# Attention's triangles masked by TensorE in PSUM instead of by GpSimd behind the exponential

## The chip, the core and the metric

One core of a Trainium2 chip runs the kernel. The metric is device time in microseconds for one execution; before the change the median of three runs is 384.74 us (384.6 to 386.14).

## What is computed

The reference is a transformer block with two parts, both on one sequence of 2048 tokens of width 512. Only the attention part matters for this change:

```python
def _A_ref(x, wqkv, wo):
    H = 32; Dh = 16; W = 256
    q, k, v = ...                                  # x @ wqkv, 32 heads of 16
    scores = jnp.einsum('bhqd,bhkd->bhqk', q, k) * Dh ** (-0.5)
    idx = jnp.arange(S)
    mask = (idx[:, None] - idx[None, :] >= 0) & (idx[:, None] - idx[None, :] < W)
    scores = jnp.where(mask[None, None], scores, -1000000000.0)
    p = _softmax(scores, axis=-1)
    o = jnp.einsum('bhqk,bhkd->bhqd', p, v)
    return o.reshape(B, S, D) @ wo                 # heads side by side

h = _layernorm(x) * (1 + ca) + sa
x = x + ga * _A_ref(h, A_wqkv, A_wo)
h = _layernorm(x) * (1 + cb) + sb
x = x + gb * _B_ref(h, B_w1, B_b1, B_w2, B_b2)     # layernorm, matmul over tokens, gelu, matmul
```

Each query sees itself and the 255 keys before it. In blocks of 128 tokens, a block of keys is seen by three blocks of queries: its own (the lower triangle), the next one (all of it) and the one after that (the opposite triangle).

## The kernel before

The kernel runs in three stages. Up to 48 us it normalizes and transposes the tokens, makes V for all heads and Q and K for the first 8 of 32 heads. From 48 to about 246 us runs attention, in an order written out by hand (`tc.manual_schedule()`), and between its steps the Q and K projections of the other 24 heads. The rest adds the residual and runs the second part, where a scheduler sets the order.

Attention is cut into 96 units: 8 sets of 4 heads (hs), 4 groups of 512 queries (tg), 3 kinds (ui). A unit has up to three pieces of keys by queries, in UNITS: (key block, first query block behind it, number of query blocks, place in the tile). Together they fill 512 columns for each head, and 128 for kind 0 of the first group (tg 0). The scores of a unit's four heads are made in two halves, a = 0 and 1, each in a tile `pss` of two PSUM banks, one bank to a head; there are three such tiles. K of a head stands in 32 rows of KeT or KoT, so a score matmul uses 32 rows of the array, and the two heads of a half use different rows.

The exponential (`emit_exp`, ScalarE, L320) reads one `pss` of 128x1024 and writes half of `et`. GpSimd then zeroes the triangles in `et` (`emit_mask`, L335): two selects a unit, one for each of the two triangles, and one alone for kind 0 of the first group (no block behind the diagonal there); MASKED names the blocks. The values (`emit_av`, L352) come one unit later: four heads side by side, 32 columns of the array each, 512 columns of `et` for each head, into the tile `psb`. After kind 2 VectorE transposes `psb` (L362), divides by the sums and merges the heads.

The loop over units u puts on TensorE: scores of unit u + 1, half 0; where `fill` has one, half of a projection (two matmuls of 128x512 into another `psb`, L387); scores of u + 1, half 1; values of u - 1. A half of scores waits for the exponential that frees its `pss`. `fill` has 48 parts for the first 69 steps; after every second one VectorE copies the projection out (L393 for Q; L395 and twice L397 for K). There are two `psb` buffers for values and projections.

Of the kernel before, what the change touches and what calls it, by code (L numbers as in the profile page):

```python
# [10 lines left out]
ALU = mybir.AluOpType  # L11

P = 128
# [10 lines left out]
SCORE_SCALE = DH ** -0.5  # L24
GELU_C0 = 0.044715
GELU_C1 = 1.5957691216057308


@with_exitstack
def kernel(  # L30
# [14 lines left out]
    nc = tc.nc  # L45
# [17 lines left out]
    identity = const.tile([P, P], DT.bfloat16, name="identity")  # L63
# [8 lines left out]
        out=mask_even[:], in_=ident_v[:, :, 0, :], axis=mybir.AxisListType.XY, op=ALU.add,  # L72
# [3 lines left out]
        out=mask_odd[:], in_=ident_v[:, :, 1, :], axis=mybir.AxisListType.XY, op=ALU.add,  # L76
# [11 lines left out]
    with tc.tile_pool(name="modps", bufs=2, space=bass.MemoryType.PSUM) as modps:  # L88
# [31 lines left out]
        for v in range(2):  # L120
            for oc in range(ND):
                col = v * ND + oc
                for k in range(ND):
                    nc.tensor.matmul(
                        ps_fm[:, col : col + 1],
                        lhsT=wmod[:, k, v * D + oc * P : v * D + (oc + 1) * P],
                        rhs=sT[:, k : k + 1],
                        start=(k == 0), stop=(k == ND - 1),
# [113 lines left out]
    for v, dst, add1 in ((2, bc_ga, False), (4, bc_cb1, True), (3, bc_sb, False), (5, bc_gb, False)):  # L242
        ps_b = ps_big.tile([P, D], DT.float32, name="psb")
        for k in range(ND):
            nc.tensor.matmul(
                ps_b[:], lhsT=sT_rep[:, k, :], rhs=wmod[:, k, v * D : (v + 1) * D],
                start=(k == 0), stop=(k == ND - 1),
# [14 lines left out]

    MASKED = ((1, 4, 0), (1, 3, 1), (0, 3, 1))

    maskLD = const.tile([P, 4, P], DT.bfloat16, name="maskLD")
    nc.vector.memset(maskLD[:], 1.0)
    nc.gpsimd.affine_select(
        out=maskLD[:, 0:2, :], in_=maskLD[:, 0:2, :], pattern=[[0, 2], [-1, P]],
        compare_op=ALU.is_ge, fill=0.0, base=-1, channel_multiplier=1,
    )  # L270
    nc.gpsimd.affine_select(
        out=maskLD[:, 2:4, :], in_=maskLD[:, 2:4, :], pattern=[[0, 2], [1, P]],
        compare_op=ALU.is_ge, fill=0.0, base=0, channel_multiplier=-1,
    )

    wod = const.tile([P, ND, D], DT.bfloat16, name="wod")
# [1 line left out]
    for g in range(ND):  # L278
        dma.dma_start(out=wod[:, g, :], in_=wo_v[:, g, :])
    nc.vector.tensor_tensor(  # L280
        out=wod[:], in0=wod[:], in1=bc_ga[:].unsqueeze(1).to_broadcast([P, ND, D]),
# [3 lines left out]
    with tc.tile_pool(name="epool", bufs=4) as epool, tc.tile_pool(  # L285
# [4 lines left out]
        units = [(hs, tg, ui) for hs in range(8) for tg in range(NT // 4) for ui in range(3)]  # L290
        merge_tiles = [None] * 4
        state = {}

        def pieces(tg, ui):
            return [(4 * tg + kb, r0, nr, blk) for kb, r0, nr, blk in UNITS[ui] if 4 * tg + kb >= 0]

        def emit_scores(u, a):
            hs, tg, ui = units[u]
            g8, par = hs // 2, hs % 2
            Ksel = KeT[g8] if par == 0 else KoT[g8]  # L300
            pss = ps_s.tile([P, 2, 4 * P], DT.float32, name="pss")
            for kb, r0, nr, blk in pieces(tg, ui):
                for jj in range(2):
                    j = 2 * a + jj
                    rows = slice(32 * j, 32 * j + 32)
                    nc.tensor.matmul(  # L306
                        pss[:, jj, blk * P : (blk + nr) * P],
                        lhsT=Ksel[rows, kb * P : (kb + 1) * P],
                        rhs=QT[g8][rows, (kb + r0) * P : (kb + r0 + nr) * P],
                        start=True, stop=True, tile_position=(32 * j, 0),  # L310
                    )
            state[u, a] = pss

        def emit_exp(u, a):
# [6 lines left out]
                out=et[:, 2 * a : 2 * a + 2, b0 * P :], in_=state.pop((u, a))[:, :, b0 * P :],  # L321
                func=ACT.Exp, scale=SCORE_SCALE,
            )

        def emit_mask(u):
            hs, tg, ui = units[u]
            et = state[u, "e"]
            lo, hi, m0 = MASKED[ui]
            if tg == 0 and ui == 0:
                lo, m0 = 3, 2  # L330
            for b0, b1, diag in ((lo, lo + 2 - m0, False), (max(lo, lo + 2 - m0), hi, True)):
                if b0 >= b1:
                    continue
                nb, s = b1 - b0, 1 if diag else -1
                nc.gpsimd.affine_select(  # L335
                    out=et[:, :, b0 * P : b1 * P], in_=et[:, :, b0 * P : b1 * P],
                    pattern=[[0, 4], [0, nb], [s, P]], compare_op=ALU.is_ge, fill=0.0,
                    base=0 if diag else -1, channel_multiplier=-s,
                )

        def emit_av(u):
            hs, tg, ui = units[u]
# [60 lines left out]
        fill = [part for g8 in range(1, ND) for tg in range(NT // 4) for part in proj_parts(g8, tg)]  # L403
# [4 lines left out]
        for u in range(len(units)):  # L408
            emit_exp(u, 0)
            if u + 1 < len(units):  # L410
                emit_scores(u + 1, 0)
            evac = None

            if fill and (n_fill - len(fill)) * (3 * 24 - 3) <= u * n_fill:
                mms, evac = fill.pop(0)
                mms()
            emit_exp(u, 1)
            if u + 1 < len(units):
                emit_scores(u + 1, 1)
            if u > 0:  # L420
                emit_av(u - 1)
            if evac is not None:
                evac()
            emit_mask(u)
        emit_av(len(units) - 1)
        assert not fill

# [45 lines left out]
    with tc.tile_pool(name="xp2", bufs=3) as xp2:  # L473
        B1_LAG = 2
        for tb in range(NT):
# [3 lines left out]
            for g in range(ND):  # L479
                nc.tensor.matmul(  # L480
                    pa[:], lhsT=OTd[g][:, tb * P : (tb + 1) * P], rhs=wod[:, g, :],
                    start=(g == 0), stop=False,
# [13 lines left out]
                out=nb2[:], in0=mv[:, 0:1], scalar=-1.0, in1=rstd[:], op0=ALU.mult, op1=ALU.mult,  # L496
# [3 lines left out]
                out=xn2[:], in_=x2[tb][:], func=ACT.Identity, bias=nb2[:], scale=rstd[:],  # L500
# [14 lines left out]
                out=nb3[:], in0=mv3[:, 0:1], scalar=-1.0, in1=rstd3[:],  # L515
# [3 lines left out]
                out=hb[tb][:], in_=h2[:], func=ACT.Identity, bias=nb3[:], scale=rstd3[:],  # L519
# [14 lines left out]
    with tc.tile_pool(name="gtmp", bufs=2) as gtmp:  # L534
# [7 lines left out]
        for fg in fgroups[2:]:  # L542
            nfc = len(fg)
            pu = ps_u.tile([P, 2, D], DT.float32, name="pu")
            for sc in range(NT):
# [3 lines left out]
                for i, fc in enumerate(fg):  # L549
                    nc.tensor.matmul(  # L550
                        pu[:, i, :], lhsT=w1r[:, sc, fc * P : (fc + 1) * P], rhs=hb[sc][:],
                        start=(sc == 0), stop=(sc == NT - 1),
# [61 lines left out]
```

## Time and profile before

| | |
|---|---|
| median of three runs | 384.74 us |
| profiled execution, its own time | 385.87 us |
| its span, first to last instruction | 383.9 us |
| attention with projections | 48.4 to 197.2 us |
| attention without projections | 197.2 to 245.5 us |
| TensorE busy over the span | 337.2 us |
| ScalarE busy over the span | 256.5 us |
| GpSimd busy over the span | 156.2 us |

The span is the time from the first to the last instruction; the profiled execution's own time is 2.0 us longer. PE is TensorE's matmuls, PEld its weight loads, ACT ScalarE, DVE VectorE, POOL GpSimd. A matmul's duration in the rows holds its drain, which runs beside the next matmul; the pace of TensorE is therefore read from the starts of successive groups, not from durations. The granted clock is a share of 2.4 GHz; its two levels here are 1.00 (2.4 GHz) and 0.50 (1.2 GHz).

### The profile page before, as it was taken

How to read it: one execution, taken by the hardware profiler on the slowest of the kernel's cores; microseconds unless marked ns; L12 is line 12 of the kernel's file. 1: busy time of each engine (PE TensorE's matmuls, PEld its weight loads, DVE VectorE, ACT ScalarE, POOL GpSimd, SP SyncE). 2: the span in 40 equal slices, each digit the busy share in tenths (PEclk: the TensorE clock that was granted, in tenths of full speed). 3: DMA queues.
4: the chain of work that ended last, by engine and by line, in shares of the span. 5: the costliest groups of instructions: out<-in, count | busy, mean ns of one | idle time of the engine just before them, and what ended most of it. 6: DMA issues, size and time to landing. Idle time of an engine off the chain costs nothing.

```text
span 383.9 us, 6976 instructions
## 1 busy us (share of the span) xinstructions
PE 337.2 (88%) x2753; PEld 131.7 (34%) x2753; DVE 208.4 (54%) x508; ACT 256.5 (67%) x350; POOL 156.2 (41%) x208
## 2 busy tenths in 40 slices
PE   0798979999999789899998989889984999899992
PEld 0544432323333222232333334233431444344441
DVE  6695635656443443535463134399983985442144
ACT  3478389799797877787999999889974653200000
POOL 9000068687776665665877878600000000000000
PEclk9999985555555555555555555699998899999997
DMA  7980000000000000000000000069302960000111
GB/s 226 364 178 1 2 0 2 3 2 0 2 2 2 1 3 2 0 2 3 0 2 2 2 3 2 0 224 406 138 0 94 402 272 2 0 31 26 56 55 55
DMA packets 17160, 24.57 MB, mean 64 GB/s; under 512 B 5096, under 2 KB 12776, under 8 KB 17128
## 3 DMA queue, kind: packets, MB, share of 16 engines
q1 hardware_dynamic: 17128, 24.13, 18.1%
q8 instruction: 21, 0.34, 0.4%
q14 instruction: 11, 0.09, 0.1%
HBM read 22.03 MB, written 2.10 MB: 63 GB/s over the span
## 4 chain that ended last, share of the span: by engine, by line
PE 56%; DVE 19%; ACT 10%; issue 3%; POOL 2%; DVEq 0%; POOLq 0%; ACTq 0%
PE pss L306 13%; PE py L570 13%; PE psb L387 10%; PE psb L352 10%; PE pu L550 8%; ACT et L320 7%; DVE ln_stats L506 3%; DVE t L362 2%; POOL et L335 2%; DVE ln_stats L487 2%; DVE merge L370 2%; DVE h L503 1%; DVE h L504 1%; DVE OTd L375 1%; PE psb L221 1%
## 5 line engine op out<-in xcount | busy, mean ns | idle before, releaser
L320 ACT ACTIVATE et<-pss 128x1024 bf16<-128x1024 f32 (+1 forms) x192 | 173.3, 1002 | 30.1 <-PE pss L306 26.2
L335 POOL TENSOR_SCALAR_AFFINE_SELECT et<-et 128x512 bf16<-128x512 bf16 (+1 forms) x184 | 147.2, 822 | 90.5 <-ACT et L320 88.5
L362 DVE STREAM_TRANSPOSE t<-psb 128x512 f32<-128x512 f32 x32 | 22.9, 717 | 90.8 <-PE psb L352 90.8
L352 PE MATMUL psb<-et,VaugT 128*32 128x128 bf16 (+1 forms) x960 | 58.7, 350 | 5.5 <-POOL et L335 1.8
L387 PE MATMUL psb<-h1T,wqkv 128*128 128x512 bf16 x96 | 48.1, 603 | 5.1 <-DVE QT L393 1.6
L570 PE MATMUL py<-guT,w2r 128*128 128x512 bf16 x224 | 48.5, 379 | 1.4 <-ACT gelu_a L456 1.4
L306 PE MATMUL pss<-QT,KoT 32*128 32x256 bf16 (+1 forms) x480 | 48.5, 352 | 1.4 <-ACT et L320 0.8
L306 PE MATMUL pss<-QT,KeT 32*128 32x256 bf16 (+1 forms) x480 | 45.9, 340 | 3.2 <-ACT et L320 2.0
L352 PEld LDWEIGHTS <-VaugT 128*32 128x32 bf16 x960 | 21.3, 113 | 40.2 <-issue 27.2
L570 PEld LDWEIGHTS <-w2r 128*128 128x128 bf16 x224 | 21.9, 98 | 28.0 <-issue 1.8
L306 PEld LDWEIGHTS <-KoT 32*128 32x128 bf16 x480 | 17.4, 114 | 40.9 <-issue 38.8
L449 PE MATMUL pu<-hb,w1r 128*128 128x512 bf16 x96 | 24.2, 392 | 7.6 <-ACT hb L518 7.3
L306 PEld LDWEIGHTS <-KeT 32*128 32x128 bf16 x480 | 17.3, 112 | 38.9 <-issue 36.7
L550 PE MATMUL pu<-hb,w1r 128*128 128x512 bf16 x128 | 29.3, 393 | 1.4 <-ACT gelu_a L456 1.4
L577 DVE SCALAR_TENSOR_TENSOR o<-bc_gb,b2FM,py 128x512 bf16<-128x512 bf16 x16 | 11.2, 744 | 32.3 <-PE py L570 32.3
L221 PE MATMUL psb<-wqkv,h1T 128*128 128x512 bf16 x64 | 17.5, 402 | 2.2 <-ACT QT L165 1.0
L480 PE MATMUL psb<-wod,OTd 128*128 128x512 bf16 x64 | 18.1, 394 | 1.2 <-ACT x L485 0.7
L550 PEld LDWEIGHTS <-w1r 128*128 128x128 bf16 x128 | 12.9, 101 | 18.2 <-issue 3.1
L370 DVE TENSOR_TENSOR merge<-t,zr 128x256 bf16<-128x256 f32 x32 | 17.8, 556 | 1.1
L449 PEld LDWEIGHTS <-w1r 128*128 128x128 bf16 x96 | 9.5, 99 | 21.3 <-issue 11.8
L468 ACT ACTIVATE gelu_sg<-gelu_inner 128x512 bf16<-128x512 bf16 x14 | 8.8, 629 | 11.3 <-DVE gelu_inner L464 11.3
L460 DVE SCALAR_TENSOR_TENSOR gelu_sq<-gelu_a 128x512 bf16<-128x512 bf16 x14 | 9.7, 690 | 10.3 <-ACT gelu_a L456 10.1
(86 smaller groups left out, 317.7 us busy)
## 6 DMA issues: line engine op xcount, KB each, us to landing
w1r<-in_B_w_dram SPq DMA_DIRECT2D x16, 448.0 KB, 9.1
w2r<-in_B_w_dram SPq DMA_DIRECT2D x14, 512.0 KB, 9.0
wmod<-in_w_mod_dram SPq DMA_DIRECT2D x6, 512.0 KB, 5.6
x<-in_A_x_dram SPq DMA_DIRECT2D x16, 128.0 KB, 4.5
out_dram<-otile SPq DMA_DIRECT2D x16, 128.0 KB, 1.7
wqkv<-in_A_wqkv_dram SPq DMA_DIRECT2D x4, 384.0 KB, 5.7
wod<-in_A_wo_dram SPq DMA_DIRECT2D x4, 128.0 KB, 3.3
c<-in_c_dram SPq DMA_DIRECT2D x1, 1.0 KB
```

Of the source, the lines that this page charges most:

```text
L221: nc.tensor.matmul(pv[:], lhsT=h1T[:, dc, tb * P : (tb + 1) * P], rhs=wqkv[:, dc, 2 * D : 3 * D], start=(dc == 0), stop=(dc == ND - 1),)
L306: nc.tensor.matmul(pss[:, jj, blk * P : (blk + nr) * P], lhsT=Ksel[rows, kb * P : (kb + 1) * P], rhs=QT[g8][rows, (kb + r0) * P : (kb + r0 ...
L320: nc.scalar.activation(out=et[:, 2 * a : 2 * a + 2, b0 * P :], in_=state.pop((u, a))[:, :, b0 * P :], func=ACT.Exp, scale=SCORE_SCALE,)
L335: nc.gpsimd.affine_select(out=et[:, :, b0 * P : b1 * P], in_=et[:, :, b0 * P : b1 * P], pattern=[[0, 4], [0, nb], [s, P]], compare_op=ALU. ...
L352: nc.tensor.matmul(po[32 * j : 32 * j + 32, q0 : q0 + nr * P], lhsT=vaug_lhsT(kb, 8 * g8 + 2 * j + par), rhs=et[:, j, blk * P : (blk + nr) ...
L362: nc.vector.transpose(out=t2[:], in_=po[:])
L370: nc.vector.tensor_tensor(out=mtv[:, :, par * DH : (par + 1) * DH], in0=t2v[:, :, 0:DH], in1=zr[:].to_broadcast([P, 16, DH]), op=ALU.mult,)
L387: nc.tensor.matmul(box[0][:], lhsT=wqkv[:, dc, col0 : col0 + P], rhs=h1T[:, dc, tok], start=(dc == 0), stop=(dc == ND - 1),)
L449: nc.tensor.matmul(pu[:, i, :], lhsT=w1r[:, sc, fc * P : (fc + 1) * P], rhs=hb[sc][:], start=(sc == 0), stop=(sc == NT - 1),)
L480: nc.tensor.matmul(pa[:], lhsT=OTd[g][:, tb * P : (tb + 1) * P], rhs=wod[:, g, :], start=(g == 0), stop=False,)
L550: nc.tensor.matmul(pu[:, i, :], lhsT=w1r[:, sc, fc * P : (fc + 1) * P], rhs=hb[sc][:], start=(sc == 0), stop=(sc == NT - 1),)
L570: nc.tensor.matmul(py[:, tl, :], lhsT=w2r[:, fc, tb * P : (tb + 1) * P], rhs=guT[fc][:], start=(fc == 0), stop=(fc == NF - 1),)
```

## The change

The tile maskLD held ones with zeros in the triangles, and nothing used it; now it holds 0 with -1e9 in the triangles that are to be masked. For each half of a unit's scores, and each of its two heads, one matmul with the identity as the stationary operand adds 2 or 3 blocks of maskLD (256 or 384 columns; 128 for kind 0 of the first group) to the scores in PSUM. For half 0 it stands behind the score matmuls, for half 1 ahead of them. The first of a bank's matmuls starts the sum, the others add. `emit_mask` and its 184 selects on GpSimd go, and the values wait for the exponential alone.

```diff
     maskLD = const.tile([P, 4, P], DT.bfloat16, name="maskLD")
-    nc.vector.memset(maskLD[:], 1.0)
+    nc.vector.memset(maskLD[:], 0.0)
     nc.gpsimd.affine_select(
         out=maskLD[:, 0:2, :], in_=maskLD[:, 0:2, :], pattern=[[0, 2], [-1, P]],
-        compare_op=ALU.is_ge, fill=0.0, base=-1, channel_multiplier=1,
+        compare_op=ALU.is_ge, fill=NEG, base=-1, channel_multiplier=1,
...
-            for kb, r0, nr, blk in pieces(tg, ui):
+            lo, hi, m0 = MASKED[ui]
+            if tg == 0 and ui == 0:
+                lo, m0 = 3, 2
+
+            def masks():
+                for jj in range(2):
+                    nc.tensor.matmul(
+                        pss[:, jj, lo * P : hi * P], lhsT=identity[:],
+                        rhs=maskLD[:, m0 : m0 + hi - lo, :],
+                        start=(a == 1), stop=(a == 0), skip_group_check=True,
+                    )
+
+
+            if a == 1:
+                masks()
+            ps = pieces(tg, ui)
+            for n, (kb, r0, nr, blk) in enumerate(ps):
                 for jj in range(2):
...
-                        start=True, stop=True, tile_position=(32 * j, 0),
-                    )
+                        start=(a == 0 and n == 0), stop=(a == 1 and n == len(ps) - 1),
+                        tile_position=(32 * j, 0), skip_group_check=True,
+                    )
+            if a == 0:
+                masks()
             state[u, a] = pss
...
-        def emit_mask(u):
...
             if evac is not None:
                 evac()
-            emit_mask(u)
```

On TensorE, in a step with a projection, the program before has score matmuls (pss, from Q and K), the projection (psb from wqkv), and score matmuls again:

```order
L306 MATMUL pss<-QT_196,KeT_200 128x256
L387 LDWEIGHTS wqkv
L387 MATMUL psb<-h1T,wqkv 128x512
...
L306 LDWEIGHTS KeT_200
L306 MATMUL pss<-QT_196,KeT_200 128x256
...
L352 LDWEIGHTS VaugT
L352 MATMUL psb<-et,VaugT 32x128
```

Scores, projection, scores, values: four shapes in a row, each unlike the one before it.

The same step after the change, a unit of kind 1, with the line numbers of the changed kernel:

```order
L324 MATMUL pss<-QT_196,KeT_200 128x256
L310 LDWEIGHTS identity
L310 MATMUL pss<-maskLD,identity 128x256
...
L392 LDWEIGHTS wqkv
L392 MATMUL psb<-h1T,wqkv 128x512
...
L310 LDWEIGHTS identity
L310 MATMUL pss<-maskLD,identity 128x256
L324 LDWEIGHTS KeT_200
L324 MATMUL pss<-QT_196,KeT_200 128x256
...
L357 LDWEIGHTS VaugT
```

The masks stand on both sides of the projection, two matmuls on each side. In a step without a projection the two halves of scores stood next to each other; now the four mask matmuls stand between them:

```order
L324 MATMUL pss<-QT_196,KeT_200 128x256
L310 LDWEIGHTS identity
L310 MATMUL pss<-maskLD,identity 128x384
...
L324 LDWEIGHTS KeT_200
L324 MATMUL pss<-QT_196,KeT_200 128x128
```

The second half's scores no longer follow the first half's directly.

On ScalarE the exponentials of the first units stand among the copies of the stage before (VaugT and QT), three of them before the change:

```order
L320 ACTIVATE et<-pss 128x2x128
L165 ACTIVATE QT_196<-psb 128x512
L320 ACTIVATE et<-pss 128x2x128
L320 ACTIVATE et<-pss 128x1024
L226 ACTIVATE VaugT<-psb 128x32x16 x2
L165 ACTIVATE QT_196<-psb 128x512
L320 ACTIVATE et<-pss 128x1024 x21
```

and two of them after it:

```order
L341 ACTIVATE et<-pss 128x2x128
L166 ACTIVATE QT_196<-psb 128x512
L341 ACTIVATE et<-pss 128x2x128
L227 ACTIVATE VaugT<-psb 128x32x16 x2
L166 ACTIVATE QT_196<-psb 128x512
L341 ACTIVATE et<-pss 128x1024 x22
```

Unit 1's first half has moved behind the last copy of Q.

## Rows read from the trace of the kernel before

**Rows 1.** The page's strips: 40 equal slices of the span, in tenths.
```profile
PE   0798979999999789899998989889984999899992
...
PEclk9999985555555555555555555699998899999997
```

**Rows 2.** Table by stage: us, busy us of each engine (instructions), PEclk, DMA.
```profile
48.40:197.20 148.80, 139.83 (x1456) 45.52 (x1455) 70.66 (x124) 124.96 (x136) 104.62 (x131) 0.52 0.01 1
197.20:245.50 48.30, 43.32 (x545) 17.04 (x541) 18.60 (x35) 46.63 (x53) 40.05 (x51) 0.50 0.01 2
```

**Rows 3.** Line L387, the projections: duration ns min/median/max, first and last start.
```profile
L387 PE MATMUL psb<-h1T,wqkv x96: 377/607/635, 48.5 to 196.3; 128*128 128x512 bf16 x96
```

**Rows 4.** Groups by line, 49-197 us, then 197-245.6: busy us, mean ns, idle before.
```profile
L320 ACT ACTIVATE et<-pss 128x1024 bf16<-128x1024 f32 x126 | 121.6, 1032 | 25.5 <-PE pss L306 21.9 <-POOL et L335 0.8
L320 ACT ACTIVATE et<-pss 128x256 bf16<-128x256 f32 x10 | 3.8, 387 | 2.9 <-PE pss L306 2.7
...
L320 ACT ACTIVATE et<-pss 128x1024 bf16<-128x1024 f32 x50 | 46.6, 1111 | 1.7 <-PE pss L306 1.6
```

**Rows 5.** Timeline of ScalarE near attention's end: start us, us, what.
```profile
227.08 18.44 ACT L320 ACTIVATE et<-pss 128x1024 bf16<-128x1024 f32 x20 [0.37 <-PE pss L306]
```

**Rows 6.** Timeline of TensorE at half clock: a step without, one with a projection.
```profile
103.65 0.62 PE L306 MATMUL pss<-QT,KeT 32*128 32x256 bf16 x8
104.20 0.62 PE L352 MATMUL psb<-et,VaugT 128*32 128x128 bf16 x12
104.75 0.61 PE L306 MATMUL pss<-QT,KeT 32*128 32x128 bf16 x6
105.29 1.03 PE L387 MATMUL psb<-h1T,wqkv 128*128 128x512 bf16 x2
106.26 0.61 PE L306 MATMUL pss<-QT,KeT 32*128 32x128 bf16 x6
106.80 0.62 PE L352 MATMUL psb<-et,VaugT 128*32 128x256 bf16 x12
107.34 0.61 PE L306 MATMUL pss<-QT,KeT 32*128 32x256 bf16 x6
```

**Rows 7.** Timeline of TensorE at full clock: transposes, scores and values, the last stage.
```profile
18.04 0.39 PE L207 MATMUL pt<-identity,xn 128*128 128x128 bf16 x4
...
51.44 0.39 PE L306 MATMUL pss<-QT,KeT 32*128 32x256 bf16 x6
51.77 0.43 PE L352 MATMUL psb<-et,VaugT 128*32 128x256 bf16 x8
...
328.54 48.51 PE L570 MATMUL py<-guT,w2r 128*128 128x512 bf16 x224 [1.41 <-ACT gelu_a L456]
```

**Rows 8.** Table of 2 us stretches about the changes of the clock; columns as rows 2.
```profile
52.00:54.00 2.00, 1.68 (x22) 0.60 (x17) 0.19 (x1) 2.00 (x4) 1.63 (x2) 1.00 0.00 0
54.00:56.00 2.00, 1.57 (x32) 0.81 (x31) 1.38 (x3) 2.00 (x4) 1.83 (x3) 0.79 0.00 0
...
244.00:246.00 2.00, 2.00 (x12) 0.48 (x8) 0.71 (x1) 1.52 (x2) 1.51 (x3) 0.50 0.00 0
246.00:248.00 2.00, 1.32 (x11) 0.32 (x10) 0.46 (x1) 1.07 (x2) 1.38 (x2) 0.93 0.00 0
...
286.00:288.00 2.00, 1.41 (x6) 0.58 (x6) 1.93 (x5) 1.02 (x2) 0.00 (x0) 1.00 0.00 0
288.00:290.00 2.00, 0.27 (x3) 0.10 (x2) 0.85 (x7) 1.57 (x4) 0.00 (x0) 1.00 0.00 0
...
294.00:296.00 2.00, 2.00 (x6) 0.61 (x5) 0.00 (x0) 0.00 (x0) 0.00 (x0) 0.52 0.59 145
```

**Rows 9.** VectorE's masked copies of K: in attention, and ahead of it.
```profile
L397 DVE TENSOR_SCALAR KeT<-KoT,mask_even x12: 353/693/1255, 58.6 to 197.7; 128x512 bf16<-128x512 bf16 x12
...
L173 DVE TENSOR_SCALAR KeT<-KoT,mask_even x4: 334/353/354, 24.0 to 44.9; 128x512 bf16<-128x512 bf16 x4
```

**Rows 10.** Timeline of ScalarE behind its last exponential.
```profile
246.91 0.60 ACT L485 ACTIVATE x<-psb 128x512 bf16<-128x512 f32 x1 [1.39 <-PE psb L484]
```

More of the change, by code (lines that the diff above doesn't have):

```diff
@@ L26 @@
 GELU_C1 = 1.5957691216057308
+NEG = -1e9
 @with_exitstack
@@ L272 @@
         out=maskLD[:, 2:4, :], in_=maskLD[:, 2:4, :], pattern=[[0, 2], [1, P]],
-        compare_op=ALU.is_ge, fill=0.0, base=0, channel_multiplier=-1,
+        compare_op=ALU.is_ge, fill=NEG, base=0, channel_multiplier=-1,
     )
@@ L323, in emit_exp @@
             )
-        def emit_mask(u):
[L326 to L338, printed above, removed]
-                )
         def emit_av(u):
```

## The prediction

> **What bounds the kernel now.** First the page's two strips [rows 1]: TensorE is busy almost throughout, and its granted clock is half (5) from slice 7 to slice 25 (9.6 us each), nearly all of the attention stage. The table by stage cuts that stage in two [rows 2]. From 48.4 to 197.2 us the projections of the later heads are spread among the attention steps (their first and last matmuls start at 48.5 and 196.3, 96 in all, two to a step, so in 48 of 69 steps) [rows 3]; TensorE is busy for 139.8 of 148.8 us. From 197.2 to 245.5 there are no projections, 26 units are left, and ScalarE is busy for 46.6 of 48.3 us. ScalarE's own rows say the same [rows 4]: before 197 us its exponentials stood idle for 25.5 + 2.9 us, nearly all behind the score matmuls of L306; after it for 1.7. So **TensorE at half clock bounds the first part, ScalarE the second**. ScalarE's pace is 18.44 us for 20 exponentials, 0.92 each, 1.84 a unit [rows 5]. GpSimd's selects are on neither bound; what they hold up is small, so their going is worth little by itself, and the question is what 384 more matmuls cost TensorE.
>
> **The pace of TensorE.** At half clock [rows 6]: a step with a projection runs from 104.75 to 107.34, 2.59 us: scores 0.54, projection 0.97, scores 0.54, values 0.54. A step without one runs from 103.65 to 104.75, 1.10 us, because both score groups (eight matmuls under one line) run over one another on different rows of the array. 48 x 2.59 + 21 x 1.10 = 147.4; five of the 69 units hold 128 columns a group in place of 512, which takes off 4.8; 142.6 against 148.8 leaves 6.2 us of waits. At full clock [rows 7]: 224 matmuls of 512 columns take 48.51 us, 0.217 each; a score group starts at 51.44 and the value group behind it at 51.77, 0.33 for 512 columns, so a change between the three shapes costs 0.11 (0.54 - 0.43 = 0.11 to 0.12 at half clock too).
>
> **The masks' price.** A unit of kind 0 or 2 gets 4 matmuls of 384 columns, one of kind 1 gets 4 of 256; with the short ones of the first block that is 122,880 columns, 240 times 512. At full clock 240 x 0.217 = **52 us**; at half clock, with (0.97 - 0.12) / 2 = 0.425 for 512, **102 us**. No row shows such a matmul in between; these are the two ends, and which of them holds is a matter of the clock alone.
>
> **Which clock.** TensorE enters attention at full clock. It loses it at about 55 us [rows 8], after four us in which it was busy for only 1.68 and 1.57 of each 2, mostly with 32-row score tiles and 32-column value tiles, while ScalarE was never idle; from then on it is the bound and stays at half, busy or not. It got the full clock back at about 246 us, while L480's full-array matmuls of 512 columns ran among the last value groups. Later, with full-array matmuls only, it kept the full clock through 286 to 290 us, busy for 1.41 and 0.27 of each 2, and lost it at 294 us. So time busy is not what decides; full-array matmuls held it at a low busy share where half-filled tiles did not at a high one. The masks are full-array matmuls. At ScalarE's pace they add 0.58 us to each unit of 1.84 from the first step on (8 x 0.217 over three units), beside 0.43 of projection in two steps of three and 0.22 of values, whose four tiles fill the array side by side. That is 1.09 of 1.84 in the first part and 0.80 in the second, where 286 to 290 us had 1.68 of 4, and the scores come on top. I take **full clock, held from 48 to the end of attention**.
> The Trainium skill (TensorE: Matmul & The Clock Gate, section "Why this matters for your kernels") says that a TensorE kept continuously busy runs at the full clock. The trace disagrees: 139.8 of 148.8 us busy at a granted 0.52. If busy time alone set the level, as the page has it, at the level that these rows show, the masks would change nothing about the clock; what that gives is the first rival's time.
>
> **The sum.** A new step is scores, masks, [projection], masks, scores, values: four changes of shape, 0.46, with a projection or without, since the masks stand on either side of it; three groups of 512 columns 0.65; masks 0.58. That is 1.69, and 2.12 with a projection (0.43).
> - First part: 69 x 1.69 + 48 x 0.43 = 137.3; the five small units take off 4.6 (1152 columns of scores and values and 1024 of masks each): 132.7. ScalarE's floor there is 64 x 1.84 + 10 x 0.39 = 122, so TensorE is still the bound, closely. Of the 6.2 us of waits I keep 5: the copies of K that free the projection's bank get shorter, since VectorE's masked copy takes 0.69 in the median (up to 1.26) where GpSimd works and 0.35 before it does [rows 9]. 137.7 against 148.8: **-11.1**. With all of the waits gone it is -16; with changes of shape at 0.15 in place of 0.115 it is -1.4.
> - Second part: 1.69 is under ScalarE's 1.84, so ScalarE stays the bound; of its 1.7 us idle about 1 goes: **-1**.
> - Start: the exponential of unit 1's first half, which ScalarE runs at 39 us now, comes behind the projection stage, but its masks stand ahead of the projection that waits for a bank; later start between 0 and 0.9, I take **+0.2**.
> - End: the last values needn't wait for GpSimd. But the first residual's copy waited 1.39 us for L484 [rows 10], and in the new order that still stands behind the last value groups: **0**, with 2 either way for the stage after, whose order on ScalarE changes a little.
> - GpSimd's 184 selects: off the path, hidden behind TensorE and ScalarE: **0**.
> In all -11.9. The profiled execution was 385.87 us, 1.1 over the median of 384.74; taken from the median the forecast is **372.8 us**.
>
> **Rivals.**
> 1. *The clock stays at half.* Price: masks in the first part (23 x 8 - 10) x 0.425 = 74; the 21 steps without a projection lose the overlap of their two score groups and gain a change, 1.75 against 1.10, 14; in the second part a unit takes 1.75 + 1.13 = 2.88 against ScalarE's 1.84, 26 units, less 3.6 for two small ones, 71 against 48.3, 23. In all +111: **495 us**, slower. It decides if identity times triangle, mostly zeros, doesn't raise the clock, or busy time alone counts. For it: half clock over 190 us of a nearly full TensorE. Against: the stretch of 286 to 290 us.
> 2. *The clock holds only while there are projections* and falls in the last 26 units: -11 in the first part, +23 in the second: **397 us**. Against it: masks alone are 0.58 of each 1.84 there.
> 3. *ScalarE becomes the bound throughout*: all of its 25.5 + 2.9 + 1.7 us of idle time goes: **355 us**. It needs TensorE under 1.84 a unit in the first part; the sum has 1.92.
> 4. *The identity's load is exposed*, about 0.1 for each of 384 matmuls: the first part gains 28 and the second 26 x 0.25 = 6.5: **407 us**, and break-even at 0.04. Against it: four full-array matmuls of 128 columns, with a load each, take 0.39 us with their drain [rows 7], and the masks are two to three times as long.
>
> **How the numbers follow.** Forecast 0.80, rival 1 0.09, rival 2 0.03, rival 3 0.03, rival 4 0.05. The forecast's bounds: -16 - 1.7 - 2 - 2 at best, 363; changes of shape at 0.15, full waits and +2 behind attention at worst, about 384, of which I keep 382. Range **362 to 382 us**, about 0.8. A measurement of this kernel tells 0.5% from no change, 1.9 us: faster 0.83, same 0.04, slower 0.13.
>
> **What would show it.** PEclk 9 in all slices of attention; the table by stage with TensorE busy at a granted 1.00 and the first part near 138 us, the second near 47; the exponentials' idle time behind score or mask matmuls down from 28 us to about 17; the mask matmuls back to back in 0.16 (384 columns) or 0.11 (256). Wrong would be: half clock anywhere between 55 us and the last exponential (rivals 1, 2), loads idle ahead of the masks (rival 4), or a first part that misses 138 us by more than 6 at full clock (the price of a change of shape).

## The result, and the profile after

The changed kernel takes 368.32 us (median; 367.99 to 368.69), beside 385.44 for the kernel before on the same chip: a ratio of 0.956, 95% interval 0.9525 to 0.9586. The forecast was 372.8 us, in a range of 362 to 382. The sign, the range and the clock were right; the gain, 17.1 us, is 5 larger than forecast.

The strips of the page of the changed kernel, as [rows 1]:

```profile
PE   0788999999999998999999999898948998999992
...
PEclk9999999999999999999999999999998999999998
```

The granted clock is 9 in every slice of attention, where slices 7 to 25 showed 5. The table by stage of the changed kernel, as [rows 2]:

```profile
48.40:183.00 134.60, 131.05 (x1739) 62.65 (x1738) 60.90 (x123) 124.37 (x137) 0.00 (x0) 1.00 0.01 2
183.00:230.70 47.70, 46.05 (x653) 21.30 (x650) 17.03 (x34) 46.01 (x53) 0.00 (x0) 1.00 0.01 2
```

Columns: stretch, its length, busy time of TensorE, weight loads, VectorE, ScalarE and GpSimd with instructions, granted clock, the DMA engines' share and GB/s. The stretch with projections is 134.6 us instead of 148.8, at a granted 1.00. In it TensorE stands idle for 134.60 - 131.05 = 3.5 us, where it was 9.0. The exponentials' groups in the same two stretches, as [rows 4]:

```profile
L341 ACT ACTIVATE et<-pss 128x1024 bf16<-128x1024 f32 x127 | 121.7, 1032 | 8.7 <-PE pss L310 4.6 <-PE pss L324 2.8
L341 ACT ACTIVATE et<-pss 128x256 bf16<-128x256 f32 x10 | 3.7, 389 | 1.6 <-PE pss L324 0.9 <-PE pss L310 0.6
...
L341 ACT ACTIVATE et<-pss 128x1024 bf16<-128x1024 f32 x49 | 45.3, 1134 | 0.6 <-PE pss L310 0.6
```

ScalarE's idle time (behind the second bar) falls from 25.5 + 2.9 to 8.7 + 1.6 us in the first stretch (about 17 us were forecast) and from 1.7 to 0.6 in the second. TensorE's timeline of the changed kernel, a step without a projection and one with it, as [rows 6]:

```profile
98.42 0.39 PE L324 MATMUL pss<-QT,KeT 32*128 32x256 bf16 x4
98.75 0.61 PE L310 MATMUL pss<-maskLD,identity 128*128 128x256 bf16 x4
99.29 0.39 PE L324 MATMUL pss<-QT,KeT 32*128 32x256 bf16 x4
99.61 0.41 PE L357 MATMUL psb<-et,VaugT 128*32 128x128 bf16 x12
99.95 0.39 PE L324 MATMUL pss<-QT,KeT 32*128 32x128 bf16 x6
100.27 0.50 PE L310 MATMUL pss<-maskLD,identity 128*128 128x384 bf16 x2
100.61 0.60 PE L392 MATMUL psb<-h1T,wqkv 128*128 128x512 bf16 x2
101.04 0.49 PE L310 MATMUL pss<-maskLD,identity 128*128 128x384 bf16 x2
101.46 0.39 PE L324 MATMUL pss<-QT,KeT 32*128 32x128 bf16 x6
...
102.12 0.39 PE L324 MATMUL pss<-QT,KeT 32*128 32x256 bf16 x6
```

By starts, the step without a projection takes 99.95 - 98.42 = 1.53 us (1.69 were reckoned, for a mean unit; this one is of kind 1, with 256 columns a mask) and the one with a projection 102.12 - 99.95 = 2.17 (2.12 were reckoned for a mean unit; this one has 384 columns a mask). No idle time stands ahead of a mask in these lines.

For the comparisons attention is cut at its exponentials: the **first part** runs from the start of the exponential of unit 1's second half to that of unit 69's first half, the **tail** from there to the end of the last exponential. The time is the median of the kernel's executions, the other columns are from the trace of one of them; e3, e4, e7 and e12 were executed once. All are us; "half clock" is where the granted clock shows 0.50 within these parts.

| kernel | time | first part | tail | half clock in attention |
|---|---|---|---|---|
| before | 385.44 | 146.65 | 49.42 | from 55.2 on |
| after | 368.32 | 132.75 | 48.11 | none |
| e1_no_mask | 381.26 | 145.11 | 48.42 | from 55.8 on |
| e2_both | 371.39 | 136.43 | 49.03 | none |
| e3_quarter | 377.11 | 140.41 | 48.31 | none |
| e4_one_head | 379.19 | 133.05 | 57.91 | 138.7-166.0, 186.5-241.1 |
| e5_masks_behind | 374.91 | 139.22 | 48.21 | none |
| e6_shared | 359.5 to 409.7 | 147.17 | 73.39 | from 133.3 on (409.7 run) |
| e7_32_rows | 393.45 | 154.06 | 52.19 | 122.9-218.5, from 232.2 on |
| e8_by_step | 420.05 | 156.39 | 73.50 | from 93.5 on |
| e9_copy_first | 364.23 | 128.19 | 48.10 | none |
| e10_shared_copy_first | 355.83 | 119.86 | 48.08 | none |
| e11_before_copy_first | 379.68 | 139.74 | 49.42 | from 50.7 on |
| e12_twice | 410.73 | 165.40 | 57.94 | none |

### The profile page after: what moved, and what is told of

Same layout as the page of the kernel before. It is cut to its first block, busy times and chain, and to the rows that moved or that the text cites. A ratio compares the mean times of both kernels' runs of the same rounds, so it can differ in the third digit from the quotient of the medians.

```text
span 366.2 us, 7468 instructions
## 1 busy us (share of the span) xinstructions
PE 328.8 (90%) x3137; PEld 152.9 (42%) x3137; DVE 198.1 (54%) x508; ACT 255.4 (70%) x350; POOL 9.1 (2%) x24
## 4 chain that ended last, share of the span: by engine, by line
PE 51%; ACT 18%; DVE 16%; issue 5%; DVEq 0%; ACTq 0%
ACT et L341 14%; PE py L574 13%; PE pss L310 9%; PE pss L324 8%; PE pu L554 8%; PE psb L357 5%; PE psb L392 4%; DVE ln_stats L510 2%; DVE t L367 2%; DVE ln_stats L491 2%; PE pu L453 2%; DVE h L507 1%; DVE h L508 1%; DVE OTd L380 1%; DVE merge L375 1%
## 5 line engine op out<-in xcount | busy, mean ns | idle before, releaser
L310 PE MATMUL pss<-maskLD,identity 128*128 128x384 bf16 (+2 forms) x384 | 79.5, 302 | 0.7 <-ACT et L341 0.3
L310 PEld LDWEIGHTS <-identity 128*128 128x128 bf16 x384 | 29.5, 97 | 33.7 <-issue 15.5
L357 PE MATMUL psb<-et,VaugT 128*32 128x128 bf16 (+1 forms) x960 | 37.5, 250 | 2.6 <-DVE KoT L400 0.8
L324 PE MATMUL pss<-QT,KeT 32*128 32x256 bf16 (+1 forms) x480 | 36.0, 245 | 0.8 <-ACT h1T L212 0.6
L324 PE MATMUL pss<-QT,KoT 32*128 32x256 bf16 (+1 forms) x480 | 36.4, 245 | 0.2 <-ACT et L341 0.2
L453 PE MATMUL pu<-hb,w1r 128*128 128x512 bf16 x96 | 24.4, 399 | 7.1 <-ACT hb L522 5.7
L392 PE MATMUL psb<-h1T,wqkv 128*128 128x512 bf16 x96 | 28.5, 379 | 1.9 <-DVE KoT L400 0.7
L554 PE MATMUL pu<-hb,w1r 128*128 128x512 bf16 x128 | 27.8, 380 | 1.4 <-ACT gelu_a L460 1.4
L357 PEld LDWEIGHTS <-VaugT 128*32 128x32 bf16 x960 | 16.6, 95 | 17.6 <-issue 14.2
L324 PEld LDWEIGHTS <-KeT 32*128 32x128 bf16 x480 | 14.8, 93 | 21.5 <-issue 19.2
L324 PEld LDWEIGHTS <-KoT 32*128 32x128 bf16 x480 | 14.9, 93 | 20.5 <-issue 18.1
```

The source lines that it names most:

```text
L310: nc.tensor.matmul(pss[:, jj, lo * P : hi * P], lhsT=identity[:], rhs=maskLD[:, m0 : m0 + hi - lo, :], start=(a == 1), stop=(a == 0), skip ...
L324: nc.tensor.matmul(pss[:, jj, blk * P : (blk + nr) * P], lhsT=Ksel[rows, kb * P : (kb + 1) * P], rhs=QT[g8][rows, (kb + r0) * P : (kb + r0 ...
L357: nc.tensor.matmul(po[32 * j : 32 * j + 32, q0 : q0 + nr * P], lhsT=vaug_lhsT(kb, 8 * g8 + 2 * j + par), rhs=et[:, j, blk * P : (blk + nr) ...
L392: nc.tensor.matmul(box[0][:], lhsT=wqkv[:, dc, col0 : col0 + P], rhs=h1T[:, dc, tok], start=(dc == 0), stop=(dc == ND - 1),)
L453: nc.tensor.matmul(pu[:, i, :], lhsT=w1r[:, sc, fc * P : (fc + 1) * P], rhs=hb[sc][:], start=(sc == 0), stop=(sc == NT - 1),)
L554: nc.tensor.matmul(pu[:, i, :], lhsT=w1r[:, sc, fc * P : (fc + 1) * P], rhs=hb[sc][:], start=(sc == 0), stop=(sc == NT - 1),)
```

## The experiments

### What the selects cost: e1_no_mask and e2_both

The kernel before with neither selects nor masks:

```diff
-            emit_mask(u)
```

> The kernel before without GpSimd's selects and without anything in their place: the triangles are left unmasked, a part of the computation is missing. Theory (the gain is TensorE's clock, the selects were hidden): the clock falls to half at the start of attention as before, the first part stays near 148 us, total 383 to 386 us, at most 2 us under the kernel before. Rival (GpSimd's selects were the cost, through the values' waits or through VectorE's slower copies): 366 to 370 us or less, as the changed kernel, since it has less work still.

Measured: 381.26 us, ratio 0.989 (0.983 to 0.994). The strip of its page:

```profile
PEclk9999995555555555555555555599999999999997
```

Without a single select the clock falls at the same place and the first part is still 145.1 us. The masks' going from GpSimd is therefore not what gave the 17 us; it is worth some 4 of them, more than the 0 of the prediction. In the traces the span is 3.2 us shorter, 1.5 of it in the first part, 1.0 in the tail and 1.0 behind attention, less 0.3 ahead of it. The changed kernel with the selects put back, behind masks that make them superfluous:

```diff
+        def emit_mask(u):
...
+            emit_mask(u)
```

> The changed kernel with GpSimd's 184 selects put back behind the exponential, so both do the masking. Theory (the gain is the full clock; the selects cost only the values' waits and VectorE's slower copies of K): full clock throughout, 1 to 3 us over the changed kernel, 369 to 372 us. Rival (the selects were a main part of the gain): 376 us or more.

Measured: 371.39 us, ratio 0.965 (0.960 to 0.970) where the changed kernel has 0.956 (0.9525 to 0.9586). In the trace the clock is full throughout attention, and the selects cost about 3 us beside the masks. Of the four executions one took 380.23 us at a mean granted clock of 0.954, where the others took 369.98 to 371.79 at 0.985 to 0.996; the ratio is that of these three, and no trace shows where the fourth lost the clock. How they do it, from the table by stage for e2_both's first part and VectorE's masked copies of K, there and then in the changed kernel (min/median/max in ns):

```profile
47.90:184.40 136.50, 128.19 (x1686) 61.34 (x1709) 72.38 (x121) 123.20 (x136) 104.74 (x129) 1.00 0.01 2
```

```profile
L418 DVE TENSOR_SCALAR KeT<-KoT,mask_even x12: 353/459/1071, 57.0 to 185.4; 128x512 bf16<-128x512 bf16 x12
L418 DVE TENSOR_SCALAR KoT<-KoT,mask_odd x12: 353/856/1219, 57.4 to 186.4; 128x512 bf16<-128x512 bf16 x12
```

```profile
L402 DVE TENSOR_SCALAR KeT<-KoT,mask_even x12: 352/353/354, 57.8 to 182.6; 128x512 bf16<-128x512 bf16 x12
L402 DVE TENSOR_SCALAR KoT<-KoT,mask_odd x12: 352/354/356, 58.2 to 183.0; 128x512 bf16<-128x512 bf16 x12
```

With selects TensorE is idle for 136.50 - 128.19 = 8.3 us of the part, as long as before the change (9.0), without them for 3.5. Between the two stands VectorE: its copies take 353 ns alone and up to 1219 beside selects. In e1, the kernel before without selects, they take 354 ns in the median and 356 at most. The Trainium skill (SBUF — State Buffer, section "Who interferes with whom") says that VectorE in a two-port mode and GpSimd lock each other out of a shared pair of ports for a whole instruction; the copies' durations agree. Who waits for the copies shows in TensorE's waits (line that waited, what it waited for: us in total, times, longest). In e2_both, first part:

```profile
PE psb L373 <- DVE KoT L416: 2.4, 3, 1.1
PE psb L373 <- DVE QT L414: 1.8, 2, 1.1
PE psb L408 <- DVE KoT L416: 1.6, 2, 0.9
PE psb L408 <- DVE QT L414: 0.9, 2, 0.7
```

and in the changed kernel:

```profile
PE psb L357 <- DVE KoT L400: 0.8, 1, 0.8
PE psb L357 <- DVE QT L398: 0.8, 1, 0.8
PE psb L392 <- DVE KoT L400: 0.7, 2, 0.4
PE psb L392 <- DVE QT L398: 0.4, 1, 0.4
```

So at the same clock the waits for one of the two `psb` buffers are 6.7 us with selects and 2.7 without. In the kernel before they come to 7.2 us, but at half clock, and 2.7 of these are for VectorE's transposes, for which e1 waits as long without any select.

### What holds the clock: e3_quarter and e7_32_rows

The prediction had put the clock down to matmuls that fill the array. e3 keeps the masks' 128 rows and all their moving columns, but uses only 32 of the identity's 128 columns, so that they fill a quarter of the array (a quarter of half 0's mask is applied; the rest, and all of half 1's, is left out):

```diff
-                        pss[:, jj, lo * P : hi * P], lhsT=identity[:],
+                        pss[0:32, jj, lo * P : hi * P], lhsT=identity[:, 0:32],
...
-                        start=(a == 1), stop=(a == 0), skip_group_check=True,
+                        start=(a == 1), stop=(a == 0), tile_position=(0, 0), skip_group_check=True,
...
-                        start=(a == 0 and n == 0), stop=(a == 1 and n == len(ps) - 1),
+                        start=(n == 0), stop=(a == 1 and n == len(ps) - 1),
```

> The changed kernel with each mask matmul cut to 32 of the identity's 128 columns: as many matmuls, as many columns streamed, a quarter of the array filled; three quarters of the mask are left out for half 0 and all of it for half 1. Theory (what fills the array holds the clock): half clock again from a few us into attention to its end, masks at 0.425 us for 512 columns, total between 470 and 510 us. Rival (TensorE's busy time, or any further matmuls, hold the clock): granted 1.00 throughout, two more changes of shape in the 48 steps with a projection, 48 x 0.22 = 11 us, total near 379 us.

Measured: 377.11 us in the one execution, full clock throughout attention:

```profile
PEclk9999999999999999999999999999996999999999
```

My theory fell: a quarter of the array's columns was enough. The 7.7 us over the changed kernel in the first part come near the two further changes of shape beside each of 48 projection halves (9.6 us at 0.10 each); where the other 1.9 went isn't shown.

e7 turns it round: 32 rows, all 128 columns, each mask issued twice (it adds the mask to 32 of the 128 keys, twice):

```diff
-                for jj in range(2):
+                for i in range(4):
+                    jj = i % 2
+                    rows = slice(32 * (2 * a + jj), 32 * (2 * a + jj) + 32)
...
-                        pss[:, jj, lo * P : hi * P], lhsT=identity[:],
-                        rhs=maskLD[:, m0 : m0 + hi - lo, :],
-                        start=(a == 1), stop=(a == 0), skip_group_check=True,
+                        pss[:, jj, lo * P : hi * P], lhsT=identity[rows, :],
+                        rhs=maskLD[rows, m0 : m0 + hi - lo, :],
+                        start=(a == 1 and i < 2), stop=(a == 0 and i > 1),
+                        tile_position=(32 * (2 * a + jj), 0), skip_group_check=True,
```

> The changed kernel with each mask matmul cut to the 32 rows of the array that its scores use, all 128 columns; two heads' matmuls run beside each other then, so each is issued twice, and TensorE is busy with masks about as long as in the changed kernel (the masks of three quarters of the keys are left out, those of the rest are added twice). e3_quarter held the full clock with all rows and 32 columns. Theory (rows that are fed hold the clock, not columns that are filled): the clock falls to half within attention, at the latest where the projections end at about 180 us, and stays there; 400 to 460 us. Rival (any matmuls that keep TensorE busy hold it): full clock, 360 to 372 us.

Measured: 393.45 us in the one execution, below the theory's 400 to 460. The strip, and the table by stage about the fall:

```profile
PEclk9999999999997555555555885599998999999998
```

```profile
119.00:123.00 4.00, 2.76 (x47) 1.57 (x50) 2.70 (x7) 3.43 (x4) 0.00 (x0) 0.99 0.01 2
123.00:127.00 4.00, 4.00 (x48) 1.58 (x42) 0.97 (x2) 2.50 (x3) 0.00 (x0) 0.50 0.01 2
```

The clock falls within attention, as the theory of fed rows said, but it doesn't stay down, and the price is lower: it holds up to 122.9 us, falls behind a stretch in which TensorE was busy for 2.76 of 4 (it waited for `psb` 1.0 and 0.5 us), comes back at 218.5 in the tail and falls once more at 232.2. So 128-row masks that fill a quarter of the array's columns kept the clock, and 32-row masks across all columns lost it; but these aren't worthless, since the kernel before, without masks, lost the clock at 55 us.

That the rows are the cause isn't shown. The 32-row masks run over one another: in a step without a projection eight of them take 0.23 us (100.42 to 100.65), where the changed kernel's four take 0.54 (98.75 to 99.29 above). Rows fed and time spent aren't told apart by these two kernels. They also differ in how still TensorE gets: in e3's stillest 4 us of the first part (146.9 to 150.9) it is busy for 3.06, in e7 for 2.76 ahead of the fall.

### How much of the masks is needed: e4_one_head, e6_shared, e8_by_step

e4 masks one of a half's two heads (the other head's mask is left out), half of the masks' work:

```diff
-                for jj in range(2):
+                for jj in range(1):
```

> The changed kernel with the mask of one of the two heads of each half: half the mask columns (the other heads' triangles are left unmasked). Theory: 0.29 us less a unit puts TensorE under ScalarE's 1.81 us in most steps; the first part falls from 134.6 us to 121 to 124, the total to 356 to 358 us, if the full clock holds. Whether it holds in the second part, where no projections help, is open: if it falls there, PEclk shows 0.50 from about 172 us and the total is 366 to 370. Rival (TensorE is not the first part's bound at full clock): no change from 368 us.

Measured: 379.19 us in the one execution, 11 more than with all masks and outside both expected ranges. The table by stage about the first fall, and TensorE's waits ahead of it (131 to 139 us):

```profile
135.00:139.00 4.00, 2.78 (x41) 1.27 (x42) 2.68 (x5) 3.44 (x4) 0.00 (x0) 0.97 0.00 0
139.00:143.00 4.00, 3.78 (x29) 1.18 (x26) 0.00 (x0) 2.80 (x3) 0.00 (x0) 0.50 0.02 4
```

```profile
PE psb L357 <- DVE KoT L400: 1.0, 1, 1.0
PE psb L357 <- DVE QT L398: 1.0, 1, 1.0
```

Half of the masks hold the clock up to 138.7 us; it falls where TensorE stood still for 1.2 of 4 us, for `psb` buffers that VectorE hadn't copied out. It comes back at 166.0 and falls again at 186.5, behind waits for `pss`, that is for ScalarE, and the tail grows from 48.1 to 57.9. Less work for TensorE made a longer kernel.

e6 leaves to GpSimd the masks of the second half of those units whose scores stand in a step with a projection (first diff); e8 gives GpSimd both halves of these units (second diff):

```diff
+                if mms is not None:
+                    by_pool.add(u + 1)
+                emit_scores(u + 1, 1, pe=mms is None)
...
+            emit_mask(u)
```

```diff
+            if fill and (n_fill - len(fill)) * (3 * 24 - 3) <= u * n_fill:
+                by_pool.add(u + 1)
```

> The changed kernel with the second half's masks of those units whose scores share a step with a projection left to GpSimd (one select for two heads); everything else is masked by TensorE. Theory (TensorE at 2.12 us a step with a projection is the first part's bound): about 1.85 there and 1.7 without, close to ScalarE's 1.81; the first part falls from 132.8 to 121 to 125 us, total 356 to 360 us at full clock. If the clock falls somewhere, as in e4_one_head: 365 to 385 us.

> Units whose scores share a step with a projection are masked by GpSimd alone, the others by TensorE. Theory: TensorE needs 1.55 us with a projection and 1.7 without, both under ScalarE's 1.81, so ScalarE is the bound throughout: first part 119 to 122 us, total 354 to 357 us, if the projections hold the full clock where there are no masks. If they don't: PEclk 0.50 in stretches of the first part, 365 to 385 us.

Measured for e6: 409.7, 372.1, 372.0 and 359.5 us in four executions of one program, with a mean granted clock of 0.822, 0.941, 0.941 and 0.991; the time follows the clock. The 359.5 and the 372 lie in the two ranges expected, the 409.7 in neither. The trace is that of the 409.7:

```profile
129.00:133.00 4.00, 2.78 (x45) 1.25 (x44) 2.95 (x6) 3.67 (x4) 2.21 (x5) 1.00 0.00 0
133.00:137.00 4.00, 3.78 (x42) 1.35 (x32) 0.48 (x2) 1.79 (x3) 1.01 (x2) 0.54 0.02 4
```

```profile
PE psb L379 <- DVE KoT L422: 1.2, 1, 1.2
...
PE psb L414 <- DVE QT L420: 0.4, 1, 0.4
```

Ahead of the fall TensorE is busy for 2.78 of 4 us; its waits from 117 to 134 us (the second fence) are for `psb` again. Behind it TensorE, at half clock and with the masks that are left, is the bound up to the last unit (a tail of 73.4 us instead of 48.1): the first rival of the prediction, entered in the middle of the kernel. e8 goes there in every execution, 420.05 us, ratio 1.093 (1.088 to 1.098), far above both of its expected times, which had left out this price:

```profile
91.00:93.00 2.00, 0.90 (x17) 0.58 (x17) 1.92 (x4) 2.00 (x4) 0.00 (x0) 1.00 0.00 0
93.00:95.00 2.00, 1.90 (x20) 0.64 (x19) 0.04 (x1) 1.72 (x3) 1.74 (x2) 0.63 0.00 0
```

Here too TensorE had been busy for only 0.90 of 2 us when the clock went, behind two waits for `psb` of 1.2 us each, and it stays at half until 277.9.

### The stillness taken away: e9, e10 and e11

If TensorE stands still for `psb`, VectorE should copy the projection out before it takes up the values' transposes. In the changed kernel (e9), in e6 (e10) and in the kernel before (e11):

```diff
-            if u > 0:
-                emit_av(u - 1)
             if evac is not None:
                 evac()
+            if u > 0:
+                emit_av(u - 1)
```

> The changed kernel, but in each step VectorE copies the finished projection out before it takes up the values' transposes (nothing is left out). Theory: what is left of the changed kernel's first part beyond TensorE's own work is TensorE waiting for a psb buffer that VectorE frees late, the copies standing behind transposes, reciprocals and products of up to several us; with the copies first the first part of attention falls from 132.8 us to 128 to 130 and the whole from 368.3 to 363 to 365.5, full clock throughout. Rival: the wait only moves, from the projection to the values (whose buffer the late transpose now frees later): 367.5 to 370, the first part 132 to 134.

Measured: 364.23 us, ratio 0.946 (0.943 to 0.949), first part 128.19, as the theory had it. In the first part TensorE waits for a `psb` once, 0.3 us, where it was 2.7; the waits and the table for that part:

```profile
PE psb L392 <- DVE KoT L400: 0.3, 1, 0.3
```

```profile
49.20:177.40 128.20, 126.47 (x1684) 61.31 (x1708) 60.29 (x121) 122.62 (x136) 0.00 (x0) 1.00 0.01 2
```

> Second half's masks of the units whose scores stand in a step with a projection by GpSimd (as in e6_shared), and the copies of the projections first (nothing is left out). Theory: e6_shared lost the full clock in some executions since TensorE stood still behind psb buffers around 130 us; with the copies first it doesn't stand still there, the full clock holds through attention, and with 0.4 us less of masks in two of three steps ScalarE is the bound: first part 119 to 123 us, the whole 353 to 358 us in every execution. Rival: the stillness has another cause, or the smaller work of full-row matmuls alone loses the clock: half clock from about 130 us on in some executions, 370 us or more, with a spread of over 10 us between them.

Measured: 355.83 us (355.11 to 356.39 in four executions), ratio 0.923 (0.9195 to 0.9265): faster than both kernels, and no execution lost the clock. The strip, the stretch about 132 us, the table by stage:

```profile
PEclk9999999999999999999999999999989999999998
```

```profile
130.00:134.00 4.00, 3.48 (x45) 1.76 (x44) 2.67 (x6) 3.67 (x7) 2.31 (x6) 1.00 0.00 0
...
49.70:169.60 119.90, 114.91 (x1599) 53.13 (x1622) 61.80 (x122) 117.91 (x136) 42.15 (x88) 1.00 0.01 2
169.60:217.60 48.00, 45.97 (x654) 20.97 (x649) 17.61 (x35) 47.35 (x55) 2.10 (x4) 1.00 0.01 2
```

Where e6 had TensorE busy for 2.78 of 4 us before it fell, e10 has 3.48 at its stillest there, and doesn't fall. ScalarE is busy for 117.9 of 119.9 us: it bounds attention now, the state that the prediction's third rival priced at 355 us.

> The kernel before with the copies of the projections ahead of the values' transposes, and nothing else (nothing is left out). Theory: the first part of before is TensorE at half clock plus some 6 us of waits, most of them for psb buffers; the copies first take off 2 to 4 us: 381 to 383.5 against 385.4, still at half clock. Rival: at half clock the waits are for ScalarE and GpSimd, and nothing changes: 384 to 386. A second rival: without the waits TensorE keeps the full clock for longer, 370 to 378.

Measured: 379.68 us, ratio 0.985 (0.982 to 0.989): 6.2 us, more than the 2 to 4 expected, and still at half clock (from 50.7 us on). So taking the waits for `psb` away doesn't hold the clock without the masks; with most of them out of the way in both kernels (1.2 us are left in e11, 0.3 in e9), the change alone is worth 379.68 - 364.23 = 15.5 us.

### The price of a change of shape, and of a mask: e5_masks_behind and e12_twice

e5 puts the masks behind the scores in the second half too, which breaks the run of masks, projection and masks into more groups:

```diff
-            if a == 1:
-                masks()
...
-            if a == 0:
-                masks()
+            masks()
```

> The changed kernel with the masks behind the scores in both halves: one more change of shape in every step, no other difference. Theory (a change of shape costs TensorE 0.11 us, and it is the first part's bound): 69 x 0.11 = 7.6 us in the first part, about 1 in the second, total 375 to 378 us. Rival (the changes are hidden by ScalarE): 368 to 369 us.

Measured: 374.91 us, ratio 0.973 (0.969 to 0.977), first part 139.22, 6.5 more than after: 6.5 / 69 = 0.094 us for each change of shape, near the 0.11, and the whole just below the 375 to 378. It also says what the place of the masks in the second half is worth.

e12 issues each mask twice:

```diff
-                for jj in range(2):
+                for jj, k in ((0, 0), (0, 1), (1, 0), (1, 1)):
```

> The changed kernel with each mask matmul issued twice in a row (the triangles get -2e9 in place of -1e9; the computation is the same). Theory: the masks cost their columns at full clock, 0.217 us for 512, and nothing else. The 69 units before the last projection have 174 x 512 columns of them, so their part grows from 132.8 us by 36 to 38, to 169 to 171; in the last 26 units TensorE passes ScalarE (2.27 us a unit against 1.84, less 2.7 for two small units), so that part grows from 48.1 to about 56; the whole 411 to 416 us. Rival: a mask matmul is dearer or cheaper in its columns than other matmuls and the most of its price is the change of shape, which a second one behind the first doesn't pay: the first part grows by less than 30 us, the whole 385 to 400.

Measured: 410.73 us in the one execution; first part +32.65, tail +9.8. TensorE's timeline, and the table for the first part:

```profile
100.73 0.82 PE L310 MATMUL pss<-maskLD,identity 128*128 128x384 bf16 x4
101.39 0.59 PE L392 MATMUL psb<-h1T,wqkv 128*128 128x512 bf16 x2
```

```profile
49.10:214.50 165.40, 164.59 (x1978) 87.03 (x1979) 60.20 (x121) 129.03 (x135) 0.00 (x0) 1.00 0.01 2
```

Four masks take 101.39 - 100.73 = 0.66 us where two took 0.34 (100.27 to 100.61 above): the second two cost 0.32, their 768 columns at 0.217 us for 512 (0.326). The rival, a price that lies in the change of shape, is out. The whole is just below its 411 to 416 us, since the first part takes 32.65 and not the 37.7 of the masks' columns: TensorE's idle time goes from 3.5 to 0.8 us, so 2.7 of them fill waits; the other 2.4 I can't place.

## Why the prediction was right, point by point

- **The bound and the clock.** TensorE at half clock bounded the first part, ScalarE the second, and the masks bring the full clock: right, and it is most of the gain (e2, which keeps the selects, is 384.36 - 371.39 = 13.0 us under the kernel before on its chip). The reason was right only in part, and that the clock held to the end was in part luck. "Full-array matmuls" is too narrow by e3 (32 of 128 columns held it), and full-array masks aren't enough by e4, whose half as many lost it. What about the masks holds the clock stays open. The stretch of 286 to 290 us, on which the prediction rested, also says less than was read from it: between 290 and 294 us, which [rows 8] leave out, TensorE nearly came to rest, and the clock fell at 294.1 us, right behind this stillness:

```profile
290.00:292.00 2.00, 1.23 (x6) 0.48 (x5) 1.47 (x3) 0.43 (x1) 0.00 (x0) 1.00 0.04 12
292.00:294.00 2.00, 0.09 (x1) 0.09 (x1) 0.58 (x4) 1.11 (x2) 0.00 (x0) 1.00 0.00 0
```

  That is what the prediction didn't see: the full clock is lost behind a stretch in which TensorE stands still, for `psb` in the first falls of e4, e6, e7 and e8, for ScalarE in the later ones of e4 and e7. e10, with the same masks as e6 and the wait made shorter, kept the clock in four of four executions, e6 in one of four. But stillness alone doesn't decide either. e2, with all of the masks, stood as still as e6 (2.78 of 4 us) and e7 (2.76) did ahead of their falls, and kept the clock in its trace:

```profile
135.70:139.70 4.00, 2.73 (x38) 1.18 (x42) 3.07 (x6) 3.54 (x4) 2.87 (x5) 1.00 0.00 0
```

  The changed kernel's stillest 4 us have 3.11, and its four executions ran at a mean granted clock of 0.992 to 0.994. That e6's executions differ, and one of e2's, shows how near the edge they are. Where the edge lies is open.
- **The masks' price.** 240 x 512 columns at 0.217 us: e12 confirms it, 0.32 us for 768 columns more. Exposed loads (rival 4) are out: two masks of 384 columns with their loads take 100.61 - 100.27 = 0.34 us, of which the columns are 0.33.
- **The first part: -13.9 for -11.1 forecast; this is the mis-sized term.** The sum was 132.7 of work and 5 us of waits kept. The table by stage, where the part goes from 148.8 to 134.6 us, has 131.05 us of work and 3.5 of waits, 134.6 in place of 137.7: both were sized too high, the work by 1.7, the waits by 1.5. That the waits went is the selects' doing: e2, which has the masks and the selects, keeps 8.3 us of idle time in the part, the changed kernel 3.5.
- **The selects at 0.** Wrong: 3 us beside the masks (e2), 4 without them (e1). The prediction did follow [rows 9] from the selects to the copies and the projection's bank, but took off only 1.2 us of waits for it, and gave the selects themselves nothing. Between e2 and the changed kernel 4.8 us of TensorE's idle time hang on them.
- **The second part: -1.3 for -1.** Right; the tail is ScalarE's in all kernels that keep the clock and issue no mask twice, 48.1 to 49.0 us.
- **The start: -0.7 for +0.2.** The first exponential already stands 0.9 us earlier (36.8 for 37.7), ahead of what the change touches. In the kernels here it varies from 35.9 to 38.0 where ScalarE's order ahead of it is the same (45.8 in e7 and 46.4 in e12), so I take it for scatter. From that exponential to the start of the first part it is 11.96 us for 11.74: the +0.2 of the forecast.
- **The end: -1.8 for 0, within the 2 given.** ScalarE's copy of the first residual waits about as long as in [rows 10]:

```profile
230.88 0.60 ACT L489 ACTIVATE x<-psb 128x512 bf16<-128x512 f32 x1 [1.24 <-PE psb L488]
```

  From there to the end it is 135.35 us for 137.02. In the other kernels with masks, whose work there is the same, it runs from 135.23 (e12) to 137.09 (e5), so that the 1.7 us are within that spread, and what makes them isn't shown.
- **The upper bound** was added up too low: with changes of shape at 0.15, all of the waits, -1, +0.2 and +2 the forecast's terms give 385.7 us, not 384. Nothing hangs on it here.

Together -0.7 - 13.9 - 1.3 - 1.8 = -17.7 us in the spans (383.9 to 366.2), -17.1 in the medians.

## What to carry to other kernels

Read the granted clock before the busy share: a TensorE that is busy for 94% of a stage can be at half speed, and moving work of another engine onto it can then make the stage shorter. Once full clock is what the kernel lives on, look for the stretches in which TensorE stands still, and mend those first; a change that spares TensorE work may lose more through the clock than it saves (e4, e8). An engine off the critical path is priced by what its instructions do to the durations of others, followed to the buffer that they free.

## What the runs showed of the hardware

- 128-row matmuls that filled 32 of the array's 128 columns held the full clock throughout attention (e3); 32-row ones across all 128 columns, twice as many, lost it at 122.9 us (e7); one execution each.
- One program ran at a mean granted clock of 0.822 to 0.991 in four executions, with times from 409.7 to 359.5 us (e6); another at 0.954 once and at 0.985 to 0.996 three times (e2).
- The selects on GpSimd stretched VectorE's 128x512 masked copies from 353 ns to a median of 459 and 856 (e2), and TensorE's waits for the buffers that VectorE frees from 2.7 to 6.7 us.
- A second mask behind the first, with a load of the same identity between them, costs its columns only: 0.32 us for two of 384.
